# Batch 1's four-token sums by whole loads and GpSimd adds behind the first stage, 112-row value loads, and the last block's columns by segments

## The chip, the cores and the metric

The kernel runs on one core of a Trainium2 chip, in one launch. The metric is the device time of one execution in microseconds (us), lower is better. Engines are named as in the profile: PE (TensorE matmuls), PEld (its weight loads), DVE (VectorE), ACT (ScalarE), POOL (GpSimd) and SP, which here only issues DMAs.

## The reference, cut to what matters

Attention over 4 batches, 8 heads, 576 tokens, 64 dimensions, followed by two gated feed-forward networks over the 2304 tokens.

```python
q_d = q.reshape(B, H, Sd, 4, D).mean(axis=3)        # sums of 4 tokens: Sd = 144
k_d = k.reshape(B, H, Sd, 4, D).mean(axis=3)
v_d = v.reshape(B, H, Sd, 4, D).mean(axis=3)
out_up = np.repeat(sm_attn(q_d, k_d, v_d), 4, axis=2)
mask = np.abs(pos[:, None] - pos[None, :]) < 4      # and attention over 7 neighbours
out_local = softmax(where(mask, scale * q @ k.T, -1e9)) @ v
x = (out_up + out_local).transpose(0, 2, 1, 3).reshape(2304, 512)
x = (silu(x @ w_gate) * (x @ w_val)) @ w_out         # 512 -> 1536 -> 512
h = x @ w_in; return (h * clip(h + 3, 0, 6) / 6) @ w_out2   # 512 -> 2048 -> 512
```

The weights arrive as 64-bit floats; q, k and v are 32-bit.

## The kernel before

**Blocks and units.** The 2304 tokens are cut into five blocks of 512, 384, 512, 512 and 384 columns (`BLOCKS = [8, 6, 8, 8, 6]` units of 64). In each block PE runs 68 units of 12 matmuls (P: 9 where the block has 384 columns): G (gate), V (value), O (output of the first network), H and P (the second), in pairs of neighbours, G0 G1 V0 V1, then G2 G3 V2 V3 O0 O1 and so on. Each fp32 factor is split into a high and a low part, and a product is three matmuls. In block 0 the weights are also loaded as 64-bit words (512 KB per unit), their upper halves are gathered by ACT (`decode_a`, line 237, tile `top`), completed by DVE (`decode_b`, line 246, tile `w`), split into high (ACT, line 264) and low (DVE, line 269, tile `wr`, once for a pair of units), and the decoded copy is stored to DRAM (`kept`) for the later blocks. `prefetch(i)` runs these steps 8, 5, 4 and 3 units ahead of the unit that PE runs. Every engine works through its own instructions in the order in which they were issued.

**The first stage (`first_batch`).** Batch 0's attention is computed before block 0 starts, in the order that the string `FRONT` writes out by hand: two letters and numbers name a step, `T`, `E`, `R` for transposes, their evacuations and sums of 4, `SC`, `M`, `W`, `N`, `PT`, `Pa`, `Pd`, `V`, `Xh`, `Xl` for the windows of 96 tokens, `d.` for the attention over the sums, `to`, `de`, `hi`, `lo` for the first weights. `fill` inserts dummy matmuls. `load_vw(i)` loads the values of a window of 102 tokens with one DMA on SP's queue (window 0 and 5 with two), and step `V` reads them. The weights `pw` of a window stand in the tile `held` (tag `x2`, one buffer) until step `PT` has transposed them.

**Sums of 4 tokens of the later batches.** Batch b's sums (`dn["q"]`, `dn["k"]`, `dn["v"]`, 72 rows for each half) are needed while block b-1 runs. For batches 2 and 3 `down_sums` loads one token of the four with a DMA on POOL's queue and adds the other three with accumulating DMAs. For batch 1 two steps of `FRONT` do it in another way for q and k: `two` loads tokens 0 and 1 (512-byte pieces of two tokens, four DMAs of 288 KB into tiles that take over the tag `fnat`), `sums` adds tokens 2 and 3 with four accumulating DMAs and then folds each pair with one GpSimd addition (line 723); v's sums are eight DMAs behind unit 25 of block 0 (`SUMV`). PE transposes q's and k's sums behind units 9, 11, 13 and 15 of block 0 (`sums_T`, line 337, tiles `pqT`, `pkT`).

**Later attention.** From batch 1 on, scores and values of the 7 neighbours are computed on DVE between the units, chunk by chunk (`chunk_scores`, lines 852 and 855; `unit_values`, from line 889), from chunk loads on SP's queue (`load_chunk`, pool `ap`, which takes over the memory of the first stage's pool `fp`). `evac` and `put_cols` write a unit's 64 columns of x into `xr`.

**Output.** `put_out` evacuates 128 tokens of a block at a time from PSUM into `os` and stores them with one DMA on SP's queue; in the last block there are three, e = 0 and 2 evacuated by ACT (line 1075) and e = 1 by DVE (line 1073). The columns of a unit are ordered by token and then by the 16 segments of 36 tokens, so the store's destination has 8 tokens outermost.

Of the kernel before, what the change touches and what calls it, by code (L numbers as in the profile page):

```python
# [43 lines left out]
SUMV = 25  # L44
# [11 lines left out]
PT0 M2 to0 N1 M3 two dP2 to1 de0 Pd0 W3 dO0 dO3 dN0 dN3 dO2 N3 dO1 Pa0 W2 dN2 dN1 sums to2 PT1  # L56
# [6 lines left out]
def tile_kernel(  # L63
# [299 lines left out]
    def first_batch():  # L363
# [6 lines left out]
        with tc.tile_pool(name="fp", bufs=1) as fp:  # L370
# [82 lines left out]
            def load_vw(i):  # L453
# [243 lines left out]

            twos = {}

            def pairs(t):  # L700
                for w, src in (("q", q), ("k", k)):
                    for half in range(2):
                        if not t:
                            st = fp.tile([TT, GT, H // 2, D], F32, tag="fnat", name=f"two{w}{half}", bufs=4)
                            st = st.rearrange("p a h d -> p (a h d)")[:NJH, :2 * H * D]
                            twos[w, half] = st.rearrange("p (h t d) -> p h t d", h=H, t=2)
                        tok = src[1, :, half * NJH * 4:(half + 1) * NJH * 4, :]
                        tok = tok.rearrange("h (j t) d -> j h t d", t=4)[:, :, t:t + 2]
                        how = {"accum_op": ALU.add} if t else {}
                        tc.keep_in_program_order(nc.gpsimd.dma_start(twos[w, half], tok, **how))  # L710

            def two():
                tc.keep_in_program_order(nc.gpsimd.tensor_copy(consts[:QT, 60:61], nm[3][:QT, 0, :1]))
                pairs(0)

            def sums():
                pairs(2)
                for w in "qk":
                    dn[w] = sp.tile([NJH, 2, H, D], F32, tag="dn" + w, name=f"dn{w}1", bufs=1)
                    for half in range(2):  # L720
                        st = twos[w, half]
                        tc.keep_in_program_order(
                            nc.gpsimd.tensor_tensor(dn[w][:, half], st[:, :, 0], st[:, :, 1], op=ALU.add)
                        )
# [11 lines left out]
            def lo(i):  # L736
# [5 lines left out]
                "Pa": Pa, "Pd": Pd, "V": V, "Xh": Xh, "Xl": Xl, "sums": sums, "two": two,  # L742
# [44 lines left out]
    first_batch()  # L787
    front[0] = False
# [111 lines left out]
    def step_x(limit):  # L900
# [12 lines left out]
        def evac():  # L913
            xf = ap.tile([P, NC, 2, 2, NSEG], F32, tag="xf", name=f"xf{gu}")
            for tp in range(2):
                for par in range(2):
                    rows = slice(par * D, par * D + D)
                    nc.vector.tensor_tensor(  # L918
                        xf[rows, :, :, tp, :].rearrange("p c j s -> p j c s"),
# [4 lines left out]
            bi = max(m for m in range(NB) if starts[m] <= gu)  # L924
            put_cols(bi, (gu - starts[bi]) * UT, xf.rearrange("p c j t s -> p c (j t s)"))
# [140 lines left out]
    def put_out(bi, e, ps):  # L1066
# [5 lines left out]
        if e % 2 and bi == NB - 1:  # L1072
# [32 lines left out]
    for bi in range(NB):  # L1105
# [34 lines left out]
        for i in range(bi * NU, (bi + 1) * NU):  # L1140
# [74 lines left out]
```

## Time and profile before

| what | value |
|---|---|
| median of 3 runs | 947.93 us (946.87 to 948.83) |
| the profiled execution's own time | 947.45 us |
| its span | 945.7 us |
| PE busy | 932.0 us (99%) |
| DVE busy | 731.7 us (77%) |
| ACT busy | 505.3 us (53%) |
| POOL busy | 105.8 us (11%) |

The span is what the profile covers; the execution's own time is 1.75 us longer. A busy share is a mean over stages: the first stage ends at about 53 us, block 0 at about 254 us, blocks 1 to 4 follow. Times in the rows are from the span's start.

### The profile page before, as it was taken

The numbers are of one execution on the slowest core, as the hardware profiler recorded it, in microseconds if no ns is written. First come the engines' busy times: TensorE is split into PE (matmuls) and PEld (weight loads), VectorE is DVE, ScalarE is ACT, GpSimd is POOL, SyncE is SP. The second block draws the span as 40 slices with busy tenths as digits, with TensorE's granted clock in tenths as the row PEclk, the third lists the DMA queues.
The fourth block names the chain that finished last, engine by engine and source line by source line (L and its number), as shares of the span: only waits on it lengthen the run. The fifth ranks groups of instructions, "written<-read, shape, count | busy, mean of one in ns | idle before, by whom it ended". The sixth has DMA issues, their size and how long they took to land.

```text
span 945.7 us, 13226 instructions
## 1 busy us (share of the span) xinstructions
PE 932.0 (99%) x4945; PEld 793.7 (84%) x4945; DVE 731.7 (77%) x1067; ACT 505.3 (53%) x945; POOL 105.8 (11%) x117
## 2 busy tenths in 40 slices
PE   8999999999999999999999999999999999999997
PEld 6887887788899988978888778888888888999996
DVE  6969989798889979998835899995447994545652
ACT  5964677877534586453335764533335445434542
POOL 6420022000153100027300000000000000000000
PEclk9999999999999999999999999999999999999999
DMA  9898899678899732579932223542232224434331
GB/s 223 174 305 314 301 347 308 192 267 295 290 239 215 163 108 69 191 219 181 200 112 89 68 90 130 196 141 91 92 109 89 89 90 131 143 128 134 131 114 34
DMA packets 100048, 160.80 MB, mean 170 GB/s; under 512 B 53368, under 2 KB 57080, under 8 KB 99984
## 3 DMA queue, kind: packets, MB, share of 16 engines
q1 hardware_dynamic: 57680, 131.43, 43.6%
q0 software_dynamic: 37408, 10.71, 10.6%
q10 hardware_dynamic: 4896, 17.83, 4.7%
q8 instruction: 39, 0.64, 0.3%
q14 instruction: 25, 0.20, 0.1%
HBM read 137.31 MB, written 22.54 MB: 169 GB/s over the span
## 4 chain that ended last, share of the span: by engine, by line
PE 72%; DVE 11%; DMA 8%; ACT 4%; issue 3%; POOL 1%; SPq 1%; ACTq 0%; POOLq 0%; DVEq 0%
PE aO L1050 15%; PE pV L358 15%; PE aP L1050 14%; PE pG L358 14%; PE pH L358 12%; DMA twok<-in_k_dram 3%; DVE wr L269 2%; DMA k<-in_k_dram 2%; DMA w<-in_moe_w_out_dram 1%; DVE pv L889 1%; DVE xf L918 1%; DVE h L1024 1%; DVE gH L1026 1%; SPq L147 1%; DVE pv L893 1%
## 5 line engine op out<-in xcount | busy, mean ns | idle before, releaser
L269 DVE TENSOR_TENSOR wr<-w,wr 128x1024 fp32r<-128x1024 f32 x170 | 207.6, 1221 | 118.0 <-ACT wr L264 117.6
L264 ACT ACTIVATE wr<-w 128x1024 fp32r<-128x1024 f32 x170 | 179.4, 1056 | 117.7 <-issue 54.1
L1050 PE MATMUL aP<-wr,gH 128*128 128x512 f32 x864 | 211.4, 395 | 1.4 <-ACT gH L1025 0.8
L358 PE MATMUL pH<-x,wr 128*128 128x512 f32 (+1 forms) x960 | 211.3, 371 | 0.7 <-DVE wr L269 0.4
L358 PEld LDWEIGHTS pH<-x,wr 128*128 128x128 f32 x960 | 173.3, 188 | 26.0 <-issue 2.1
L1050 PEld LDWEIGHTS aP<-wr,gH 128*128 128x128 f32 x864 | 159.6, 188 | 36.2 <-ACT gH L1025 1.6
L358 PE MATMUL pG<-xr,wr 128*128 128x512 f32 (+1 forms) x720 | 153.6, 368 | 0.8 <-ACT xr L309 0.8
L358 PE MATMUL pV<-xr,wr 128*128 128x512 f32 (+1 forms) x720 | 153.4, 368 | 0.9 <-ACT sl L1014 0.9
L1050 PE MATMUL aO<-gV,wr 128*128 128x512 f32 (+1 forms) x720 | 152.7, 368 | 0.0
L358 PEld LDWEIGHTS pV<-xr,wr 128*128 128x128 f32 x720 | 130.9, 188 | 18.2 <-ACT sl L1014 1.4
L358 PEld LDWEIGHTS pG<-xr,wr 128*128 128x128 f32 x720 | 130.8, 188 | 18.3 <-ACT xr L309 1.2
L1050 PEld LDWEIGHTS aO<-gV,wr 128*128 128x128 f32 x720 | 130.8, 188 | 16.7
L1023 ACT ACTIVATE h<-pH,consts 128x512 f32<-128x512 f32 (+1 forms) x80 | 51.3, 642 | 52.7 <-PE pH L358 52.5
L1025 ACT ACTIVATE gV<-sl 128x512 fp32r<-128x512 f32 (+1 forms) x60 | 35.0, 584 | 67.5 <-DVE sl L1020 67.4
L1014 ACT ACTIVATE sl<-pG 128x512 f32<-128x512 f32 (+1 forms) x60 | 33.2, 554 | 70.5 <-PE pG L358 70.4
L1025 ACT ACTIVATE gH<-h 128x512 fp32r<-128x512 f32 (+1 forms) x80 | 46.8, 586 | 44.6 <-DVE h L1024 44.4
L237 ACT ACTIVATE top<-w 128x512 f16<-128x512 bf16 x68 | 53.3, 794 | 16.6 <-DVE w L246 4.7
L852 DVE TENSOR_TENSOR pr<-q,k 128x1792 f32<-128x1792 f32 x27 | 54.5, 2019 | 9.8 <-DMA k<-in_k_dram 9.7
L1024 DVE SCALAR_TENSOR_TENSOR h<-h,pH 128x512 f32<-128x512 f32 (+1 forms) x80 | 50.5, 631 | 13.3 <-ACT h L1023 12.6
L1026 DVE TENSOR_TENSOR gH<-h,gH 128x512 fp32r<-128x512 f32 (+1 forms) x80 | 50.5, 632 | 11.6 <-ACT gH L1025 11.5
L889 DVE TENSOR_TENSOR pv<-sc,v 128x1792 f32<-128x1792 f32 x27 | 54.6, 2021 | 0.5
L855 DVE TENSOR_REDUCE sc<-pr 128x28 f32<-128x1792 f32 x27 | 54.4, 2013 | 0.2
(137 smaller groups left out, 754.1 us busy)
## 6 DMA issues: line engine op xcount, KB each, us to landing
w<-kept SPq DMA_DIRECT2D x136, 512.0 KB
kept<-w ACTq DMA_DIRECT2D x34, 512.0 KB
w<-in_moe_w_out_dram SPq DMA_DIRECT2D x28, 512.0 KB
w<-in_moe_w_in_dram SPq DMA_DIRECT2D x16, 512.0 KB
w<-in_moe_w_gate_dram SPq DMA_DIRECT2D x12, 512.0 KB
w<-in_moe_w_val_dram SPq DMA_DIRECT2D x12, 512.0 KB
out_dram<-os SPq DMA_DIRECT2D x16, 256.0 KB
dnv<-in_v_dram POOLq DMA_DIRECT2D x24, 144.0 KB, 7.1
```

The lines of the kernel that those rows point to most:

```text
L237: behind(nc.scalar.activation(halves(top[i % 2], 2, F16)[:, :, 1], h3.bitcast(BF16), AF.Copy))
L264: behind(nc.scalar.activation(parts[i][:, 0], w32[i // 2].rearrange("p u e -> p (u e)"), AF.Copy))
L269: behind(nc.vector.tensor_tensor(r[:, 1], s, r[:, 0].bitcast(F32), op=ALU.subtract))
L358: nc.tensor.matmul(ps, r[:, a, c], x[:, c, b_, :ps.shape[1]], start=part is HIGH and a == c == 0, stop=part is LOW and c == NC - 1,)
L852: nc.vector.tensor_tensor(pr, qt[:, a:a + SUB, None, :].to_broadcast([P, SUB, W, D]), win(kt, a, SUB), op=ALU.mult)
L855: nc.vector.tensor_reduce(sc[:, a:a + SUB], pr, axis=AX.X, op=ALU.add)
L889: nc.vector.tensor_tensor(pr, pe[:, a:a + SUB, :, None].to_broadcast([P, SUB, W, D]), win(vt, a, SUB), op=ALU.mult)
L1023: nc.scalar.activation(h, ps, AF.Relu, scale=1 / 6, bias=half1[:, 0:1])
L1024: nc.vector.scalar_tensor_tensor(h, h, 1.0, ps, op0=ALU.min, op1=ALU.mult)
L1025: nc.scalar.activation(g[:, 0, :nt], h, AF.Copy)
L1026: nc.vector.tensor_tensor(g[:, 1, :nt], h, g[:, 0, :nt].bitcast(F32), op=ALU.subtract)
L1050: nc.tensor.matmul(ps, **one, start=f_ == 0 and a == b_ == 0, stop=f_ == nf - 1 and b_ == 1,)
```

## The change

Batch 1's sums of 4 tokens leave `FRONT` (steps `two`, `sums`) and unit 25. A new function `whole_sums`, called right behind the first stage, loads all four tokens of a half of q, k or v with one DMA on POOL's queue (1 KB pieces, 576 KB), six in all, two of them ahead, into two halves of one tile with the tag `x2`; GpSimd then folds the four tokens with two additions per piece. The values of batch 0's windows are loaded with 112 rows where 112 fit (96 and then 3 in the last window), and rows outside the sequence are zeroed by DVE and not loaded. In the last block the columns of two neighbouring units are ordered by segment first, so that `put_out` stores with 16 segments outermost; the last 128 tokens are evacuated half by DVE, half by ACT.

```diff
-SUMV = 25
 FRONT: ... -PT0 M2 to0 N1 M3 two dP2 to1 de0 Pd0 W3 ... dO1 Pa0 W2 dN2 dN1 sums to2 PT1
            +PT0 M2 to0 N1 M3 dP2 to1 de0 Pd0 W3 ... dO1 Pa0 W2 dN2 dN1 to2 PT1
     def put_cols(bi, col, xv):
-        dst = columns(bi, col, xv)
+        dst = columns(bi, col, UT)
+        if bi == NB - 1:
+            e, r = divmod(col // UT, 2)
+            dst = columns(bi, e * P, P).rearrange("p c a (s u t) -> p c a s u t", s=NSEG, u=2)[:, :, :, :, r]
+    def whole_sums(b):
+        st = sp.tile([P, NC, 2, UMAX * UT], F32R, tag="x2", name=f"st{b}", bufs=1).bitcast(F32)
+        st = st.rearrange("p c a t -> p (c a t)")[:NJH].rearrange("p (g h t d) -> p g h t d", g=2, h=H, t=4)
+        gp = Ordered(nc.gpsimd)
+        pieces = [(w, half) for w in "qkv" for half in range(2)]
+        def load(n):
+            w, half = pieces[n]
+            src = {"q": q, "k": k, "v": v}[w][b, :, half * NJH * 4:(half + 1) * NJH * 4, :]
+            gp.dma_start(st[:, half], src.rearrange("h (j t) d -> j h t d", t=4))
+        def add(n):
+            w, half = pieces[n]
+            if half == 0:
+                dn[w] = sp.tile([NJH, 2, H, D], F32, tag="dn" + w, name=f"dn{w}{b}", bufs=1)
+            t = st[:, half]
+            gp.tensor_tensor(t[:, :, 0:2], t[:, :, 0:2], t[:, :, 2:4], op=ALU.add)
+            gp.tensor_tensor(dn[w][:, half], t[:, :, 0], t[:, :, 1], op=ALU.add)
+        load(0)
+        load(1)
+        for n in range(len(pieces)):
+            add(n)
+            if n + 2 < len(pieces):
+                load(n + 2)
             def load_vw(i):
                 if lo < 0:
-                    late(nc.sync, t[:-lo], v[0, :, :-lo, :].rearrange("h s d -> s h d"))
+                    nc.vector.memset(t[:-lo], 0.0)
                 if hi > S:
-                    late(nc.sync, t[S - lo:hi - lo], v[0, :, S - (hi - S):, :].rearrange("h s d -> s h d"))
+                    nc.vector.memset(t[QT:], 0.0)
                 a, e = max(lo, 0), min(hi, S)
-                late(nc.sync, t[a - lo:e - lo], v[0, :, a:e, :].rearrange("h s d -> s h d"))
+                m = QT if hi > S else min(QT + 16, P, S - a)
+                late(nc.sync, t[a - lo:a - lo + m], v[0, :, a:a + m, :].rearrange("h s d -> s h d"))
+                if a + m < e:
+                    late(nc.sync, t[a - lo + m:e - lo], v[0, :, a + m:e, :].rearrange("h s d -> s h d"))
...
-            def pairs(t): ...   def two(): ...   def sums(): ...
     first_batch()
+    whole_sums(1)
     def evac():
+            by = "p c (s j t) -> p c j t s" if bi == NB - 1 else "p c (j t s) -> p c j t s"
+            xs = xf.rearrange(by, j=2, t=2, s=NSEG)
...
     def put_out(bi, e, ps):
-        if e % 2 and bi == NB - 1:
+        if bi == NB - 1 and e == BLOCKS[bi] * UT // P - 1:
+            h = DM // 2
+            nc.vector.tensor_copy(os[:, :h], ps[:, :h])
+            nc.scalar.activation(os[:, h:], ps[:, h:], AF.Copy)
+        elif e % 2 and bi == NB - 1:
...
+            elif bi == NB - 1:
+                dst = flat(out, (b * S + u * 4) * DM, [[SL * DM, NSEG], [DM, 4 * m], [1, DM]])
             else:
                 dst = flat(out, (b * S + u * 4) * DM, [[DM, 4 * m], [SL * DM, NSEG], [1, DM]])
...
-            if i == SUMV:
-                last = [t for key, t in state.items() if key[0] == "g"][-1]
-                for _ in down_sums(1, ["v"], last[:, 0, :1].bitcast(F32)):
-                    pass
```

## Rows read from the trace of the kernel before

**Rows 1.** Timeline, PE: start, length, tiles, [idle before <-releaser], first stage and block 0.

```profile
48.82 0.88 PE L159 MATMUL fO<-turned,vw 102*64 102x96 f32 x16 [0.38 <-DMA vw<-in_v_dram]
...
80.59 0.41 PE L337 MATMUL pqT<-ident,dnq 72*128 72x72 f32 x4
80.81 5.71 PE L358 MATMUL pG<-xr,wr 128*128 128x512 f32 x24
...
87.66 6.07 PE L358 MATMUL pV<-xr,wr 128*128 128x512 f32 x24 [0.88 <-ACT sl L1014]
93.56 0.42 PE L337 MATMUL pkT<-ident,dnk 72*128 72x72 f32 x4
```

**Rows 2.** Busy time by stretch, block 0: length, each engine's busy us, clock, DMA share, GB/s.

```profile
54.00:90.00 36.00, 35.12 (x160) 28.90 (x159) 28.87 (x31) 20.96 (x30) 3.05 (x2) 1.00 0.93 306
90.00:122.00 32.00, 32.00 (x146) 26.06 (x146) 31.03 (x38) 20.39 (x31) 0.00 (x0) 1.00 0.88 310
```

**Rows 3.** Timeline, DVE: low halves of the weights and the first scores.

```profile
70.75 2.02 DVE L852 TENSOR_TENSOR pr<-q,k 128x1792 f32<-128x1792 f32 x1 [2.46 <-DMA k<-in_k_dram]
...
78.78 1.23 DVE L269 TENSOR_TENSOR wr<-w,wr 128x1024 fp32r<-128x1024 f32 x1
...
86.20 1.22 DVE L269 TENSOR_TENSOR wr<-w,wr 128x1024 fp32r<-128x1024 f32 x1
```

**Rows 4.** Timeline, POOL: additions of the first stage, sums of batch 1.

```profile
16.07 1.26 POOL L446 TENSOR_TENSOR spread<-spread 72x512 f32<-72x512 f32 x1 [5.95 <-DMA spread<-in_v_dram]
17.42 0.72 POOL L447 TENSOR_TENSOR fvd<-spread 72x256 f32<-72x256 f32 x1
...
29.61 1.86 POOL L710 DMA_DIRECT2D twoq<-in_q_dram  x2 [0.40 <-PE fPT L159]
...
36.41 1.41 POOL L710 DMA_DIRECT2D twoq<-in_q_dram  x1 [3.33 <-DMA twoq<-in_q_dram]
...
46.06 1.27 POOL L723 TENSOR_TENSOR dnq<-twoq 72x512 f32<-72x512 f32 x1 [1.20 <-DMA twoq<-in_q_dram]
...
61.85 1.75 POOL L723 TENSOR_TENSOR dnk<-twok 72x512 f32<-72x512 f32 x1 [1.09 <-DMA twok<-in_k_dram]
```

**Rows 5.** Timeline, DVE: instructions beside POOL's additions, and one without.

```profile
46.45 1.42 DVE L246 SCALAR_TENSOR_TENSOR w<-w,top 128x512 int32<-128x512 int32 x1
...
60.34 0.97 DVE L246 SCALAR_TENSOR_TENSOR w<-w,top 128x512 int32<-128x512 int32 x1 [2.03 <-ACT top L237]
...
62.98 1.18 DVE L246 SCALAR_TENSOR_TENSOR w<-w,top 128x512 int32<-128x512 int32 x1
...
64.69 0.68 DVE L246 SCALAR_TENSOR_TENSOR w<-w,top 128x512 int32<-128x512 int32 x1
```

**Rows 6.** Groups of DVE's instructions by line, 54 to 90 us: busy us, mean ns.

```profile
L855 DVE TENSOR_REDUCE sc<-pr 128x28 f32<-128x1792 f32 x2 | 4.0, 2010 | 0.0
...
L1020 DVE TENSOR_TENSOR sl<-sl,pV 128x512 f32<-128x512 f32 x4 | 2.7, 677 | 0.0
```

**Rows 7.** Timeline, SP: DMA issues of the values and of the first chunk.

```profile
16.02 22.06 SPq L147 DMA_DIRECT2D vw<-in_v_dram  x8
...
63.64 0.33 SPq L147 DMA_DIRECT2D q<-in_q_dram  x1
```

**Rows 8.** Timeline, ACT and SP at the end, and a 128x256 evacuation of the first stage.

```profile
53.86 0.37 ACT L159 ACTIVATE xr<-fO 128x256 fp32r<-128x256 f32 x1
...
937.20 3.32 SPq L1084 DMA_DIRECT2D out_dram<-os  x3
...
939.29 0.60 ACT L1075 ACTIVATE os<-aP 128x512 f32<-128x512 f32 x1 [2.12 <-PE aP L1050]
```

**Rows 9.** Busy time by stretch at the end, columns as in rows 2.

```profile
936.00:940.00 4.00, 3.25 (x15) 2.36 (x13) 0.69 (x1) 1.20 (x2) 0.00 (x0) 1.00 0.18 31
940.00:944.00 4.00, 0.00 (x0) 0.00 (x0) 0.00 (x0) 0.00 (x0) 0.00 (x0) 0.89 0.50 159
944.00:946.00 2.00, 0.00 (x0) 0.00 (x0) 0.00 (x0) 0.00 (x0) 0.00 (x0) 0.50 0.03 12
```

More of the change, by code (lines that the diff above doesn't have):

```diff
@@ L55 @@
 SC0 dM1 M0 Rk3 dE1 Rk2 dT0 dP0 W0 SC1 dS3 dM3 dT1 dP1 SC2 M1 dE3 W1 dS2 dT3 N0 dM2 dP3 SC3 dE2 dT2
-PT0 M2 to0 N1 M3 two dP2 to1 de0 Pd0 W3 dO0 dO3 dN0 dN3 dO2 N3 dO1 Pa0 W2 dN2 dN1 sums to2 PT1
+PT0 M2 to0 N1 M3 dP2 to1 de0 Pd0 W3 dO0 dO3 dN0 dN3 dO2 N3 dO1 Pa0 W2 dN2 dN1 to2 PT1
 Pa1 Pd1 SC5 SC4 M5 W5 PT3 V1 M4 N2 Pa3 de1 Xh1 W4 V0 Xh0 Pd3 Xl1 N5 de2 PT2 V3 Pd2 Pa2 Xl0 to3 PT5 Xh3
@@ L298, in tile_kernel, with columns @@
     x_done = [0]
-    def columns(bi, col, xv):
+    def columns(bi, col, n):
         if bi not in xr:
             xr[bi] = sp.tile([P, NC, 2, UMAX * UT], F32R, tag="xr", name=f"xr{bi}")
-        return xr[bi][:, :, :, col:col + xv.shape[2]]
+        return xr[bi][:, :, :, col:col + n]
     def put_cols(bi, col, xv):
-        dst = columns(bi, col, xv)
+        dst = columns(bi, col, UT)
+        if bi == NB - 1:
+            e, r = divmod(col // UT, 2)
+            dst = columns(bi, e * P, P).rearrange("p c a (s u t) -> p c a s u t", s=NSEG, u=2)[:, :, :, :, r]
         nc.scalar.activation(dst[:, :, 0], xv, AF.Copy)
@@ L684, in X @@
                         e = min(QT, starts[bi + 1] * UT - t0)
-                        yield bi, cs, columns(bi, t0 + a - starts[bi] * UT, ps[:, :, a:e]), ps[:, :, a:e]
+                        yield bi, cs, columns(bi, t0 + a - starts[bi] * UT, e - a), ps[:, :, a:e]
                         a = e
@@ L696, in Xl @@
                         vec.tensor_tensor(to[:, cs, 1], xv, to[:, cs, 0].bitcast(F32), op=ALU.subtract)
[L698 to L724, printed above, removed]
             def to(i):
@@ L741, in first_batch @@
                 "dN": dN, "SC": SC, "M": M, "W": W, "N": N, "PT": PT,
-                "Pa": Pa, "Pd": Pd, "V": V, "Xh": Xh, "Xl": Xl, "sums": sums, "two": two,
+                "Pa": Pa, "Pd": Pd, "V": V, "Xh": Xh, "Xl": Xl,
                 "Yh": lambda i: Xh(i, False), "Yl": lambda i: Xl(i, False), "to": to, "de": de, "hi": hi, "lo": lo,
@@ L913, in evac @@
         def evac():
-            xf = ap.tile([P, NC, 2, 2, NSEG], F32, tag="xf", name=f"xf{gu}")
+            bi = max(m for m in range(NB) if starts[m] <= gu)
+            xf = ap.tile([P, NC, UT], F32, tag="xf", name=f"xf{gu}")
+            by = "p c (s j t) -> p c j t s" if bi == NB - 1 else "p c (j t s) -> p c j t s"
+            xs = xf.rearrange(by, j=2, t=2, s=NSEG)
             for tp in range(2):
@@ L918, in evac @@
                     nc.vector.tensor_tensor(
-                        xf[rows, :, :, tp, :].rearrange("p c j s -> p j c s"),
+                        xs[rows, :, :, tp, :].rearrange("p c j s -> p j c s"),
                         px[tp * D:tp * D + D, :, :, par, :],
@@ L923, in evac @@
                     )
-            bi = max(m for m in range(NB) if starts[m] <= gu)
-            put_cols(bi, (gu - starts[bi]) * UT, xf.rearrange("p c j t s -> p c (j t s)"))
+            put_cols(bi, (gu - starts[bi]) * UT, xf.rearrange("p c (s t) -> p c s t", t=4) if bi == NB - 1 else xf)
             x_done[0] += 1
```

## The prediction

> **What bounds the kernel now.** I read the page's busy times first, then PE's timeline for its idle places, then DVE and POOL around them, then the end. PE is busy for 932.0 of 945.7 us, so a change gains or loses only at the few places where PE waits or has ended. The first is window 5's value step, 0.38 us late for its DMA [rows 1]. In block 0 there is one stall, 0.88 us before V4 at 87.66 [rows 1]. The reader should see how thin block 0's lead is: DVE is busy for 28.87 of 36 us from 54 to 90 us and for 31.03 of 32 from 90 to 122 [rows 2], and it finishes the low half of a pair of weights just before PE wants it. For the pair G4 G5 it is done at 78.78 + 1.23 = 80.01 and PE starts at 80.81; for V4 V5 it is done at 87.42 and PE starts at 87.66 [rows 1, 3]. So DVE sets PE's pace here, with a lead of 0.8 and 0.2 us. The last place is the end: PE has ended at 939.3, and the last store moves data until 944 [rows 8, 9].
>
> **The first stage.** The steps `two` and `sums` issue eight DMAs and four additions on POOL; all of it leaves. PE waits for none of these there. What PE waits for is the value load. SP needs 22.06 us to issue eight value loads [rows 7], and the last one makes PE wait 0.38 us [rows 1]. Seven loads stand there now; if they are spread better over the engines, this wait goes: -0.4. Bounds: 0 if the wait stays, -1.1 if the 0.74 us that an addition of `sums` holds DVE there (below) also counts; PE's row after row up to 48.44 shows no other wait, so I take -0.4. The two zeroings on DVE have no input and run before the first transposes have landed, and the rows beyond 102 are read by nobody: nothing.
>
> **What GpSimd's additions cost.** An addition of 512 elements takes 1.26 us, one of 256 takes 0.72 [rows 4], so 256 elements more cost 0.54, and one of 1024 is estimated at 1.26 + 2 x 0.54 = 2.34. A piece is one of 1024 and one of 512: 3.6 us, six pieces 21.6 us, in place of four additions of 1.27 (5.1 us).
>
> When: the tile has the tag of `held`, which PE reads until 48.4, so the first load is issued there. The first 288 KB load of `two` was issued at 29.61 and had landed when POOL went on at 36.41 [rows 4], 6.8 us; so the first addition begins at about 55. A piece can't follow faster than its additions and one issue (0.93, half of 1.86 in rows 4), 4.5 us, so six pieces fill 55 to 82 at best and about 55 to 90 if POOL is held up too. That is the stretch in which DVE sets the pace.
>
> How the two engines meet is shown by three instructions of line 246, both of whose inputs are in SBUF: 0.68 us alone, but 1.42 at 46.45, 0.97 at 60.34 and 1.18 at 62.98, each while an addition runs [rows 5]. The addition of 46.06 ends at 47.33, and the instruction ends 0.54 later: DVE had waited for the addition to end. It is so in the other direction too: the addition of 61.85 takes 1.75, since it waits for the line-269 instruction before it [rows 4]. The three lose 0.74 + 0.29 + 0.50 = 1.53 us to 5.1 us of additions: 30%.
>
> Bounds for 21.6 us. From below: 30% of it is 6.5; before already pays 0.8 of it behind 54 us, and DVE's wait of 2.46 us for the first chunk [rows 3] is swallowed by a late DVE (its load stood behind `sums` on SP at 63.64 [rows 7], which goes too); 3.2 stay. From above: of the 36 us from 54 to 90, DVE is idle for 7.1 and for 4.0 + 2.7 [rows 6] runs instructions that read one tile of SBUF or PSUM; the rest, 22.2 less the 0.8 of holding, is 21.4 us that exclude an addition. 21.4 + 21.6 = 43.0 us can't run side by side; with the free 13.8 us all used by additions DVE is 43.0 - 36 = 7.0 us late, with half of them used 13.9. I take 7.0: the 30% come from stretches where DVE had pauses, and against the 13.9 speaks that a held-up POOL drifts into whatever DVE leaves free. Less the lead of 0.3 (between 0.2 and 0.8, nearer the smaller, since DVE gets no pause until 122) PE is 6.7 us late; bounds 2.9 and 13.6. It isn't made up: PE's work behind it is fixed, and the stalls of before that it could swallow are 0.9 at 87.66.
>
> The Trainium skill (SBUF — State Buffer, "SBUF: two separate sides") says that DVE and GpSimd share one pair of ports under an exclusive lock, held for the whole instruction, and that a DVE instruction with two SBUF inputs needs it. The three rows agree. By that rule taken alone the lower bound would be the 7.0 of full exclusion and not 3.2; the sum above stands without it.
>
> **What else moves in block 0.** POOL's queue holds only these loads and additions; nothing else waits behind them until block 1's sums at 254. PE transposes q's sums at 80.59 and k's at 93.56 in order [rows 1]; with q done at about 65 and k at about 75 neither waits. The `x2` tile is wanted again at the end of O, over 60 us later. The same bytes of q, k and v are loaded either way, now closer together in a stretch where the DMA engines are at a share of 0.93 [rows 2]; a late DVE also asks for weights later, so I add nothing, and count it in the range. v's eight DMAs at 130 to 165 go: PE waits for none of them.
>
> **The end.** The last evacuation takes 0.60 for 512 columns [rows 8]; a 256-column one 0.37, its DVE counterpart about the same: -0.2. Then the stores: 4 us x 31 + 4 x 159 + 2 x 12 GB/s = 784 KB, the three of 256 KiB, at a share of 0.50, so with half of the 16 DMA engines [rows 9]. At that share the first 4 us hold 1.44 us of transfer, so data flow from 938.56, 1.36 behind the first issue at 937.20. If 16 segments outermost use all engines, the last store, issued at 939.7, flows from 941.06 at 318 GB/s and is through in 0.82, at 941.9 and not 944.1: -2.2 with the evacuation's 0.2. I take -2.0; bounds -0.2 (rate unchanged) and -2.4. The reordered columns cost DVE and ACT only other strides in blocks 3 and 4, where PE shows no wait: nothing.
>
> The Trainium skill (DMA: Bandwidth & Descriptors, "Why a DMA increments its semaphore by 16 and not by 1") says that a hardware-queue DMA runs on the largest number of engines up to 16 that divides the outermost size on both sides. For 8 and 128 that is 8, which the share of 0.50 agrees with; it would be 16 now, and 6 and 16 for 102 and 112 rows, which no row here shows.
>
> **Sum.** 947.45 + 6.7 - 0.4 - 2.0 = 951.75 against the profiled execution; the median of the runs is 0.48 above it: 952.2 us, 0.45% slower.
>
> **The rivals.**
> - The other side: POOL's additions fit into what DVE leaves free, and DVE is less than 0.3 us late. For it: DVE's pauses between 54 and 61, the vanished wait of 2.46, and a lock that DVE might win each time. Against it: 21.6 us don't fit into 13.8. It would give 947.9 - 2.4 = 945.5. It decides from a lateness below 2.7 (0.3 + 0.4 + 2.0): then the change is a gain. Chance of over 0.2% faster: 0.21.
> - The lateness is near its lower bound of 3.2 (1 to 4.5), and both ends cancel: 2.9 - 2.4 gives 948.4. Chance 0.18.
> - Loads or additions are so late that PE waits for k's sums at 93.56: with DMAs twice as large at the pace of rows 4 (13.6 us each, two in flight) k is done at about 84, and only a starved POOL adds more. Some 5 us on top of the forecast: 957. Chance 0.06.
> - That the stores or value loads don't spread better takes away 1.8 and 0.4 of the gain; it moves the forecast to 954.4 and lies within its range.
>
> **How the numbers follow.** The forecast, lateness from 4.5 to 13, has 0.55; its own range is 949.9 to 957. About 0.2%, 1.9 us, is what a measurement of this kernel can tell from no change. Slower is 0.55 + 0.06 = 0.61, same 0.18, faster 0.21. To leave out 2 in 10 the range goes from the other side's 945.3 to 957.
>
> **What the profile will show.** Right: additions of about 2.3 and 1.3 us on POOL from 55 to 90; instructions of lines 246, 269, 852 and 1026 lengthened beside them; PE waits before G4, V4 or O0 that sum to some 7 us; no wait at window 5; a DMA share near 1 at the end, which comes 2 us sooner behind PE. Wrong, if DVE's lengthened instructions sum to under 3 us, or if PE runs through 60 to 110 without waits.

## The result, and the profile after

The changed kernel takes 957.37 us (956.13 to 961.82 over six runs) against 948.38 of the kernel before on the same chip: a ratio of 1.0098, with an interval of 1.0073 to 1.0122. That is slower, as forecast, but by 9.0 us and not by 4.3, and 0.4 us beyond the end of the range. Ratios and their intervals are formed from undisturbed executions alone, medians from all. The profiled execution has a span of 956.8 us, 11.1 more than before: the two profiled executions (958.47 and 947.45 us) lie 2 us farther apart than the medians, and the terms below are read from these two.

PE's timeline of the changed kernel, rows with a wait and those that answer to [rows 1]; its L386 and L1056 are L358 and L1050 of before:

```profile
53.14 5.72 PE L386 MATMUL pG<-xr,wr 128*128 128x512 f32 x24
...
66.47 5.80 PE L386 MATMUL pG<-xr,wr 128*128 128x512 f32 x24 [2.18 <-DVE sl L1026]
...
79.07 5.53 PE L1056 MATMUL aO<-gV,wr 128*128 128x512 f32 x23 [1.14 <-DVE wr L268]
84.44 0.41 PE L365 MATMUL pqT<-ident,dnq 72*128 72x72 f32 x4
...
85.95 5.51 PE L386 MATMUL pG<-xr,wr 128*128 128x512 f32 x23 [0.77 <-DVE wr L268]
...
95.17 0.50 PE L386 MATMUL pV<-xr,wr 128*128 128x512 f32 x1 [3.14 <-ACT sl L1020]
98.06 7.93 PE L386 MATMUL pV<-xr,wr 128*128 128x512 f32 x23 [2.39 <-DVE wr L268]
105.83 0.41 PE L365 MATMUL pkT<-ident,dnk 72*128 72x72 f32 x4
```

Block 0 begins 0.12 us earlier than before (53.14 for 53.26), and k's first transposes, a fixed place in PE's order, come 12.27 us later (105.83 for 93.56). So block 0 has lost 12.4 us, and the whole loss is there: PE ends 12.7 us later than before, and the end behind PE, 6.45 us before, is 4.87. The five waits sum to 9.62 us, in place of the 0.88 at 87.66: 8.7 more. A further 2.4 us is in the row of 98.06: its 23 matmuls take 7.93 us, while the 23 of 85.95 take 5.51. The remaining 1.2 us are spread over PE's restarts behind the waits.

Windows of the changed kernel, columns as in [rows 2], at PE's last wait and at the end:

```profile
60.00:90.00 30.00, 25.92 (x114) 20.42 (x114) 26.25 (x21) 12.36 (x18) 20.82 (x13) 1.00 0.99 307
...
96.00:98.00 2.00, 0.00 (x0) 0.00 (x0) 2.00 (x2) 0.39 (x1) 1.92 (x2) 0.61 0.98 382
98.00:100.00 2.00, 1.94 (x5) 1.55 (x6) 2.00 (x3) 0.27 (x1) 1.15 (x1) 0.50 0.49 191
100.00:102.00 2.00, 2.00 (x6) 1.59 (x5) 2.00 (x2) 2.00 (x4) 0.00 (x0) 0.50 0.58 101
102.00:104.00 2.00, 2.00 (x7) 1.55 (x6) 2.00 (x3) 0.80 (x2) 0.00 (x0) 0.68 1.00 400
...
951.00:955.00 4.00, 0.93 (x5) 0.43 (x3) 0.72 (x2) 0.38 (x1) 0.00 (x0) 1.00 0.69 190
955.00:957.00 2.00, 0.00 (x0) 0.00 (x0) 0.00 (x0) 0.00 (x0) 0.00 (x0) 0.90 0.04 13
```

The clock column explains the slow row of 98.06. PE ran one matmul between 92.03 and 98.06, and the granted clock fell to 0.50, which is 1.2 GHz, and was back at 1.00 (2.4 GHz) from 104. The first line says that the DMA engines were full in block 0 too, at a share of 0.99 from 60 to 90 us (before, 0.93 from 54 to 90 [rows 2]). The two last lines answer to [rows 9]: a DMA share of 0.69 in the last 4 us of transfer where it was 0.50.

DVE's timeline, instructions of block 0 beside the additions (L245, L268, L856 and L1032 are L246, L269, L852 and L1026 of before), and those of 67.33 and 84.67, which ran beside none or between two:

```profile
57.49 2.43 DVE L245 SCALAR_TENSOR_TENSOR w<-w,top 128x512 int32<-128x512 int32 x1 [2.32 <-ACT top L236]
60.22 1.42 DVE L245 SCALAR_TENSOR_TENSOR w<-w,top 128x512 int32<-128x512 int32 x1 [0.29 <-ACT top L236]
61.55 4.17 DVE L268 TENSOR_TENSOR wr<-w,wr 128x1024 fp32r<-128x1024 f32 x1
...
67.33 0.68 DVE L1032 TENSOR_TENSOR gV<-sl,gV 128x512 fp32r<-128x512 f32 x1
...
75.08 2.80 DVE L856 TENSOR_TENSOR pr<-q,k 128x1792 f32<-128x1792 f32 x1 [3.53 <-DMA k<-in_k_dram]
...
84.67 1.23 DVE L268 TENSOR_TENSOR wr<-w,wr 128x1024 fp32r<-128x1024 f32 x1
85.81 2.88 DVE L1032 TENSOR_TENSOR gV<-sl,gV 128x512 fp32r<-128x512 f32 x1
...
95.38 2.63 DVE L268 TENSOR_TENSOR wr<-w,wr 128x1024 fp32r<-128x1024 f32 x1
```

POOL's timeline beside it, from five of the six pieces:

```profile
56.98 2.39 POOL L158 TENSOR_TENSOR st<-st 72x1024 f32<-72x1024 f32 x1 [5.62 <-DMA st<-in_q_dram]
59.45 1.63 POOL L158 TENSOR_TENSOR dnq<-st 72x512 f32<-72x512 f32 x1
61.38 0.83 POOL L158 DMA_DIRECT2D st<-in_k_dram  x1 [0.30 <-POOL dnq L158]
62.23 2.41 POOL L158 TENSOR_TENSOR st<-st 72x1024 f32<-72x1024 f32 x1
...
67.16 0.83 POOL L158 DMA_DIRECT2D st<-in_k_dram  x1 [0.30 <-POOL dnq L158]
72.26 2.38 POOL L158 TENSOR_TENSOR st<-st 72x1024 f32<-72x1024 f32 x1 [4.27 <-DMA st<-in_k_dram]
74.72 1.28 POOL L158 TENSOR_TENSOR dnk<-st 72x512 f32<-72x512 f32 x1
...
85.69 2.46 POOL L158 TENSOR_TENSOR st<-st 72x1024 f32<-72x1024 f32 x1 [1.57 <-DMA st<-in_v_dram]
...
97.00 2.15 POOL L158 TENSOR_TENSOR dnv<-st 72x512 f32<-72x512 f32 x1
```

Read the two together. The L1032 instruction starts at 85.81, 0.12 us behind POOL's addition of 85.69, and ends at 88.69, 0.54 us behind that addition's end (88.15), as the one at 46.45 did in [rows 5]. It took 2.88 us instead of 0.68. The Trainium skill (SBUF — State Buffer, "SBUF: two separate sides") says that whichever of the two engines starts first has the shared ports for its whole instruction. These rows agree, in both directions: a 512-element addition that finds DVE at work takes 1.63 or 2.15 us, for 1.28 at 74.72. DVE's instructions with one input from SBUF at most are not lengthened: in the stretch of the groups below L859 (one SBUF input) has a mean of 2006 ns and L1026 (one SBUF and one PSUM input) of 675, and before they had 2009 and 677.

DVE's groups of the same four lines from 53 us to the same place in PE's order (pV at 133.69, and at 121.47 before):

```profile
L245 DVE SCALAR_TENSOR_TENSOR w<-w,top 128x512 int32<-128x512 int32 x25 | 22.6, 918 | 3.9 <-ACT top L236 3.9
L268 DVE TENSOR_TENSOR wr<-w,wr 128x1024 fp32r<-128x1024 f32 x12 | 19.0, 1581 | 0.4 <-ACT wr L263 0.4
L856 DVE TENSOR_TENSOR pr<-q,k 128x1792 f32<-128x1792 f32 x5 | 10.8, 2169 | 3.5 <-DMA k<-in_k_dram 3.5
...
L1032 DVE TENSOR_TENSOR gV<-sl,gV 128x512 fp32r<-128x512 f32 x8 | 7.6, 954 | 0.0
```

They sum to 60.0 us; the same 25, 12, 5 and 8 instructions took 17.5 + 14.6 + 10.1 + 5.5 = 47.7 before. DVE is held for 12.3 us, and PE loses 12.4. That the two agree so closely is in part chance, since 2.4 of PE's 12.4 are the clock. DVE's idle time before these lines hardly changed: 3.9 + 0.4 + 3.5 = 7.8 us, and 4.6 + 0.8 + 2.5 = 7.9 before. From this profile alone one would say that the additions are the whole cause and the loads cost nothing. The experiments say otherwise.

The end, SP's issues, DVE and ACT (answers to [rows 8]):

```profile
949.87 3.50 SPq L1096 DMA_DIRECT2D out_dram<-os  x3
...
951.97 0.42 DVE L1080 COPY os<-aP 128x256 f32<-128x256 f32 x1 [0.67 <-PE aP L1056]
952.42 0.38 ACT L1081 ACTIVATE os<-aP 128x256 f32<-128x256 f32 x1 [2.58 <-DVE os L1080]
```

The two halves of the last evacuation follow each other. The last data is in SBUF 0.87 us behind PE's end, where one ACT instruction had needed 0.64.

### The profile page after: what moved, and what is told of

The parts are those of the page before. It is cut to its first block, busy times and chain, and to the rows that moved or that the text cites. A ratio compares the mean times of both kernels' runs of the same rounds, so it can differ in the third digit from the quotient of the medians.

```text
span 956.8 us, 13203 instructions
## 1 busy us (share of the span) xinstructions
PE 936.0 (98%) x4945; PEld 795.3 (83%) x4945; DVE 746.6 (78%) x1070; ACT 505.2 (53%) x945; POOL 110.0 (12%) x113
## 4 chain that ended last, share of the span: by engine, by line
PE 78%; DVE 11%; ACT 4%; issue 3%; DMA 3%; SPq 1%; ACTq 0%; DVEq 0%
PE aP L1056 16%; PE pH L386 14%; PE pV L386 14%; PE aO L1056 14%; PE pG L386 14%; DVE wr L268 3%; DMA w<-in_moe_w_val_dram 1%; DVE pv L893 1%; PE fO L158 1%; DVE xf L925 1%; DVE pv L897 1%; DVE gH L1032 1%; DVE h L1030 1%; DMA w<-kept 1%; ACT pd L764 1%
## 5 line engine op out<-in xcount | busy, mean ns | idle before, releaser
L268 DVE TENSOR_TENSOR wr<-w,wr 128x1024 fp32r<-128x1024 f32 x170 | 212.0, 1247 | 117.5 <-ACT wr L263 117.1
L386 PE MATMUL pH<-x,wr 128*128 128x512 f32 (+1 forms) x960 | 211.5, 372 | 0.8 <-DVE wr L268 0.4
L1056 PE MATMUL aP<-wr,gH 128*128 128x512 f32 x864 | 211.2, 395 | 0.8 <-DVE wr L268 0.5
L386 PEld LDWEIGHTS pH<-x,wr 128*128 128x128 f32 x960 | 173.3, 188 | 26.2 <-issue 2.1
L1056 PEld LDWEIGHTS aP<-wr,gH 128*128 128x128 f32 x864 | 159.7, 188 | 35.4 <-issue 1.6
L386 PE MATMUL pV<-xr,wr 128*128 128x512 f32 (+1 forms) x720 | 155.7, 372 | 5.5 <-ACT sl L1020 3.1
L386 PE MATMUL pG<-xr,wr 128*128 128x512 f32 (+1 forms) x720 | 154.3, 369 | 3.7 <-DVE sl L1026 2.2
L1056 PE MATMUL aO<-gV,wr 128*128 128x512 f32 (+1 forms) x720 | 153.0, 368 | 1.1 <-DVE wr L268 1.1
L386 PEld LDWEIGHTS pV<-xr,wr 128*128 128x128 f32 x720 | 132.7, 190 | 23.3 <-ACT sl L1020 3.3
L386 PEld LDWEIGHTS pG<-xr,wr 128*128 128x128 f32 x720 | 130.6, 188 | 22.2 <-issue 2.6
L1056 PEld LDWEIGHTS aO<-gV,wr 128*128 128x128 f32 x720 | 130.7, 188 | 18.2 <-DVE wr L268 1.6
L856 DVE TENSOR_TENSOR pr<-q,k 128x1792 f32<-128x1792 f32 x27 | 55.3, 2048 | 8.7 <-DMA k<-in_k_dram 8.5
L1032 DVE TENSOR_TENSOR gH<-h,gH 128x512 fp32r<-128x512 f32 (+1 forms) x80 | 50.5, 632 | 11.6 <-ACT gH L1031 11.5
L245 DVE SCALAR_TENSOR_TENSOR w<-w,top 128x512 int32<-128x512 int32 x68 | 51.6, 771 | 9.5 <-ACT top L236 6.4
```

What stands on the lines that cost most here:

```text
L245: behind(nc.vector.scalar_tensor_tensor(w32[i // 2][:, i % 2].bitcast(I32), h12, 13, top[i % 2], op0=ALU.logical_shift_right, op1=ALU.bitw ...
L268: behind(nc.vector.tensor_tensor(r[:, 1], s, r[:, 0].bitcast(F32), op=ALU.subtract))
L386: nc.tensor.matmul(ps, r[:, a, c], x[:, c, b_, :ps.shape[1]], start=part is HIGH and a == c == 0, stop=part is LOW and c == NC - 1,)
L856: nc.vector.tensor_tensor(pr, qt[:, a:a + SUB, None, :].to_broadcast([P, SUB, W, D]), win(kt, a, SUB), op=ALU.mult)
L1032: nc.vector.tensor_tensor(g[:, 1, :nt], h, g[:, 0, :nt].bitcast(F32), op=ALU.subtract)
L1056: nc.tensor.matmul(ps, **one, start=f_ == 0 and a == b_ == 0, stop=f_ == nf - 1 and b_ == 1,)
```

## The experiments

The table lists every run, with the kernel before's median on the same chip. "k at" is when PE starts k's first transposes in the profile (93.56 before, 105.83 after), and "end" the span behind PE's last matmul.

| kernel | us | before | ratio (interval) | k at | end |
|---|---|---|---|---|---|
| e1 ends only | 945.65 | 948.06 | 0.9966 (0.9947-0.9985) | 92.68 | 4.79 |
| e2 few additions | 954.60 | 948.06 | 1.0063 (1.0042-1.0085) | 101.72 | 4.79 |
| e3 additions, no loads | 958.79 | 948.06 | 1.0097 (1.0068-1.0126) | 107.06 | 4.83 |
| e4 v as before | 952.95 | 948.06 | 1.0051 (1.0032-1.0070) | 98.59 | |
| e5 early, few additions | 949.28 | 948.02 | 1.0011 (0.9992-1.0031) | 97.17 | |
| e6 early, all additions | 956.88 | 948.02 | 1.0084 (1.0062-1.0106) | 104.28 | |
| e7 a third of the additions | 949.04 | 948.02 | 1.0004 (0.9983-1.0024) | 98.24 | |
| e8 ends, ACT last | 944.14 | 948.02 | 0.9948 (0.9931-0.9965) | 92.27 | 4.64 |
| e9 early q and k, few additions | 944.28 | 946.69 | 0.9974 (0.9964-0.9984) | 92.43 | |
| e10 values only | 946.11 | 946.69 | 0.9996 (0.9987-1.0005) | 91.77 | 6.57 |
| e11 last block only | 945.98 | 946.69 | 0.9996 (0.9979-1.0013) | 93.00 | 4.55 |
| e12 two half stores | 944.47 | 946.69 | 0.9977 (0.9963-0.9992) | | 4.36 |

**e1, the change without the new sums.** The rest of the change stays; `two`, `sums` and the v step of before return.

```diff
-    whole_sums(1)
+    # FRONT has "two" and "sums" again, the loop its SUMV step
```

> The changed kernel with batch 1's sums put back as before (steps two and sums in the first stage, v's accumulating DMAs behind unit 25); the 112-row value loads, the last block's columns and the split last evacuation stay. Theory L (GpSimd's additions hold DVE up while they run) and theory D (the six whole loads crowd the DMA engines, so weights and the first chunk come late) both put the whole loss in the sums: 946.3 to 947.2, 1.2 to 2.1 us below before, of which 1.6 at the end (from 6.45 us to 4.87 between PE's end and the span's end) and 0.1 in the first stage. Theory E (the reordered columns or the value loads cost something in blocks 3 and 4 or in the first stage): 950 or more.

It gains: 2.4 us by the medians. PE has no wait in block 0. So the new sums cost 957.37 - 945.65 = 11.7 us by the medians (12.5 by the two ratios), and not the 6.7 of the forecast.

**e2, the loads without the additions.** The additions run on one of 64 elements of each head; the rest of the sums is a constant, so the kernel leaves most of the sums out.

```diff
-gp.tensor_tensor(t[:, :, 0:2], t[:, :, 0:2], t[:, :, 2:4], op=ALU.add)
-gp.tensor_tensor(dn[w][:, half], t[:, :, 0], t[:, :, 1], op=ALU.add)
+gp.tensor_tensor(t[:, :, 0:2, :1], t[:, :, 0:2, :1], t[:, :, 2:4, :1], op=ALU.add)
+gp.tensor_tensor(dn[w][:, half, :, :1], t[:, :, 0, :1], t[:, :, 1, :1], op=ALU.add)
...
+    gp.memset(dn[w], 0.01)
```

> The changed kernel, but GpSimd adds only one of the 64 dimensions of each piece (16 and 8 elements per row and not 1024 and 512); the sums are otherwise a constant that GpSimd writes before the first load, so most of the sums is left out. All six whole loads stay, with their waits. L: DVE is no longer held, PE's waits between 60 and 100 us go to under 2 us and the clock stays at 2.4 GHz: 946.3 to 948.5. D: the loads are as before, so weights and the first chunk are still late: 953 or more.

That additions are the whole cause fell here: the loads alone cost 9.0 us over e1. DVE is no longer held (a mean of 687 ns for L245, where the changed kernel has 918), but waits. DVE's timeline of e2 has the first chunk of k:

```profile
76.23 2.03 DVE L857 TENSOR_TENSOR pr<-q,k 128x1792 f32<-128x1792 f32 x1 [6.28 <-DMA k<-in_k_dram]
```

DVE's timeline of e1, the same instruction:

```profile
69.90 2.03 DVE L884 TENSOR_TENSOR pr<-q,k 128x1792 f32<-128x1792 f32 x1 [1.80 <-DMA k<-in_k_dram]
```

SP's timelines, the issue of that load, in e2:

```profile
61.69 0.44 SPq L146 DMA_DIRECT2D k<-in_k_dram  x1
```

and in e1:

```profile
62.19 0.42 SPq L147 DMA_DIRECT2D k<-in_k_dram  x1
```

So from the issue to the use of k it is 14.5 us in e2 and 7.7 in e1.

ACT's timeline of e2, the longest wait for weights:

```profile
81.66 0.79 ACT L236 ACTIVATE top<-w 128x512 f16<-128x512 bf16 x1 [7.66 <-DMA w<-in_moe_w_gate_dram]
```

Windows of e2, before the loads and in them:

```profile
30.00:50.00 20.00, 20.00 (x268) 18.21 (x267) 17.88 (x43) 17.60 (x77) 0.69 (x1) 1.00 0.52 157
...
60.00:90.00 30.00, 24.75 (x100) 19.06 (x99) 18.09 (x21) 12.08 (x17) 5.01 (x13) 0.94 1.04 322
```

The DMA engines are half idle from 30 to 50 us and full from 60 to 90 (the share is a mean that can come out above 1). The rate, 322 GB/s, is that of e1 in the same stretch (317), so nothing is slower; other bytes move. The DMA queues from 60 to 90 us (packets, MB, share), SP's in e1:

```profile
q1 hardware_dynamic: 2901, 6.87, 69.6%
```

SP's and POOL's in e2:

```profile
q1 hardware_dynamic: 2103, 5.40, 58.9%
q0 software_dynamic: 818, 2.30, 27.7%
```

SP's queue brings block 0's own k chunk and weights, and 1.5 MB less of them gets through beside the 2.3 MB of POOL's loads; in e1 POOL's queue moves nothing there. One thing is not as in the changed kernel: without additions POOL issues its last load at 75.16 and not at 83.29, so the loads stand closer together, and 9.0 us is their price at that pace. The clock adds to it: after a wait of 2.14 us, 23 matmuls at 79.44 take 7.14 us.

**e3, the additions without the loads.** e1, with twelve additions of the same sizes on a tile of zeros, back to back from 63.72 us (in the changed kernel they are spread from 57 to 99); their result is read by nobody.

```diff
...
+gp.memset(st[:, 0], 0.0)
+for n in range(6):
+    t = st[:, 0]
+    gp.tensor_tensor(t[:, :, 0:2], t[:, :, 0:2], t[:, :, 2:4], op=ALU.add)
+    gp.tensor_tensor(st[:, 1, :, 0], t[:, :, 0], t[:, :, 1], op=ALU.add)
```

> e1_ends_only with twelve GpSimd additions of the sizes of the change (six of 1024, six of 512 elements per row) on a scratch tile of zeros behind the first stage, with no load: extra work that nothing reads, about 22 us on GpSimd from 64 us on. L: DVE's two-input instructions beside them are held for 8 to 12 us, PE waits as much less its lead: 953 to 957. D: nothing waits for these additions and no byte more is moved: within 0.7 us of e1_ends_only.

The additions alone cost 13.1 us over e1 (958.79, above the 953 to 957 expected), with a DMA share of only 0.42 and 0.29 from 70 to 90 us. DVE has no idle time from 70 to 100. DVE's timeline of e3, one of L269's:

```profile
79.40 3.38 DVE L269 TENSOR_TENSOR wr<-w,wr 128x1024 fp32r<-128x1024 f32 x1
```

POOL's timeline of e3, all twelve:

```profile
63.72 28.84 POOL L159 TENSOR_TENSOR sti<-sti 72x1024 f32<-72x1024 f32 x12
```

Unhindered they would take 6 x (2.38 + 1.28) = 22.0 us by the rows above, so POOL is held for 6.8 us as well.

9.0 and 13.1 sum to 22.1, and the two together cost 11.7 to 12.5. They overlap: while DVE is held it would have waited for its data anyway, and its wait for k is 3.53 us in the changed kernel where e2 has 6.28. By these runs the pair costs no more than the additions alone.

**e4, v as before.** Only q and k are loaded whole and added.

```diff
-pieces = [(w, half) for w in "qkv" for half in range(2)]
+pieces = [(w, half) for w in "qk" for half in range(2)]
+# and the SUMV step of before for v
```

> The changed kernel with v's sums as before (accumulating DMAs behind unit 25), so four pieces and not six: 14.6 us of additions, which end at about 83 us. L: in the changed kernel DVE's holding before 83 us made PE some 5 us late (PE waits 2.2, 1.1 and 0.8 up to 86, the larger ones behind it), and the clock doesn't fall: 950.5 to 953. D: four of six loads, which stand just as close together: 953 to 955.

Two thirds of the pieces cost 1.0051 - 0.9966 = 0.85% of 948 us, 8.1 us, and the last third 4.4. Within the intervals the cost follows the number of pieces, so it isn't the one late piece that the third rival spoke of.

**e5, e2's loads in the first stage.** Quarters of 4 heads go through the tiles of before's `two`, four loads ahead, from 32 us on; the additions are cut, and most of the sums left out, as in e2.

```diff
+quarters = [(w, half, hh) for w in "qkv" for half in range(2) for hh in range(2)]
 ...
 def two():
+    ...
+    for n in range(4):
+        load_q(n)
 def sums():
+    for n in range(12):
+        add_q(n)
+        if n + 4 < 12:
+            load_q(n + 4)
```

> e2_few_adds with the same bytes in the same 1 KB pieces loaded earlier: twelve loads of half the size on POOL's queue, in the first stage from 29 us on, four ahead, into the tiles that two used; GpSimd adds only one of 64 dimensions and the rest of the sums is a constant, so most of the sums is left out. Theory D1 (e2's loss of about 9 us against e1_ends_only comes from where the loads stand: from 49 to 85 us the DMA share is full and the first chunk and the weights queue beside them, while from 30 to 50 us the share is 0.4 to 0.6): 945.5 to 949. Theory D2 (loads of this kind on POOL's queue cost that much wherever they stand): 952 or more.

Of the 9.0 us, 4.3 stay (1.0011 - 0.9966), and DVE still waits 4.3 us for k. This time it is not the transfer of k. The quarters stand in memory of the first stage's pool, which the chunk's tiles take over, so SP waits 6.3 us for v's last quarter to land, at 67.7 us, and 0.9 us for POOL to read it, before it can issue the chunk. SP's timeline of e5:

```profile
69.28 0.42 SPq L147 DMA_DIRECT2D k<-in_k_dram  x1
```

That is 7.1 us later than in e1, and the weights behind it in SP's queue are late with it; from issue to use k takes 5.2 us here, less than e1's 7.7.

**e6, e5 with all additions.**

```diff
-t = whole.pop(n)[:, :, :, :1]
+t = whole.pop(n)[:, :, :, :64]
...
```

> e5_early_few_adds with all additions (24 on GpSimd of 512 and 256 elements per row, about 24 us, from 36 us on), so the complete sums. If only the place of the loads mattered: within 1 us of e5_early_few_adds. L: the additions hold DVE in the first stage, where it is busy for 9 of 10 us, and behind it, and the first chunk's load waits for the last addition: 951 to 958.

The additions cost 6.9 us on top of e5 (1.0084 - 1.0011). On 12 x (1.27 + 0.72) = 23.9 us of additions that is 29%, in a kernel that already waits. Moving them does not hide them, since DVE's work is on PE's path in the first stage too. PE's timeline of e6:

```profile
47.54 0.54 PE L159 MATMUL fPT<-ident,held 96*102 96x96 f32 x4 [1.88 <-DVE turned L159]
```

The first stage ends 5.3 us later than in e1 (its last transposes begin at 58.16, not 52.83), and of the 11.6 us by which k's transposes are late only 6.3 arise in block 0, where SP can issue the chunk of k only at 76.35, behind the last addition.

**e7, a third of e3's additions.** The 1024-element ones are left out, six of 512 stay.

```diff
-gp.tensor_tensor(t[:, :, 0:2], t[:, :, 0:2], t[:, :, 2:4], op=ALU.add)
```

> e3_adds_no_loads with only the six smaller of the twelve additions that nothing reads (512 elements per row): about 8 us on GpSimd from 64 us on and not 21.6. L, with DVE's lateness in proportion to the additions (e3_adds_no_loads was 13 us over e1_ends_only for 28.8 us on POOL): 949 to 951. If DVE's lead and its pauses swallow this much: within 1 us of e1_ends_only.

6 x 1.28 = 7.7 us of additions cost 1.0004 - 0.9966 = 0.38%, 3.6 us, that is 47%; e3's 22.0 us cost 12.4 by the ratios, 56%. The 3.6 us are uncertain by some 2.7, so a free third is excluded, and a smaller free amount is not.

**e9, e5 for q and k alone**, v as before, which tells apart what is left in e5.

```diff
-quarters = [(w, half, hh) for w in "qkv" for half in range(2) for hh in range(2)]
+quarters = [(w, half, hh) for w in "qk" for half in range(2) for hh in range(2)]
```

> e5_early_few_adds for q and k alone (eight loads and not twelve, the last landed at about 58 us), v's sums as before by accumulating DMAs; GpSimd adds one of 64 dimensions of q and k, the rest of these sums is a constant, so most of them is left out. D1: e5_early_few_adds was still 3.6 us over e1_ends_only because its v loads stood from 50 to 68 us, where the DMA share was 1.0; without them 945.5 to 946.5, as e1_ends_only. If the remaining 3.6 us come from the loads of q and k: 948.5 or more.

The remainder is gone: k's transposes stand at 92.43, as in e1, and SP issues the chunk of k at 61.90. Windows of e9 in the same two stretches as e2's:

```profile
30.00:50.00 20.00, 20.00 (x269) 18.21 (x268) 18.21 (x43) 17.70 (x78) 11.05 (x22) 1.00 0.98 224
...
60.00:90.00 30.00, 29.76 (x137) 24.30 (x136) 27.56 (x29) 18.08 (x28) 0.00 (x0) 1.00 0.93 317
```

q's and k's whole loads cost nothing from 31 to 53 us, where the DMA engines have room without them (e2's first line). Behind the first stage the six loads cost 9.0 us (e2). v's whole loads at a place where nothing waits for them or for their memory were not run.

**e10 and e11, the two other parts alone.** e10 is the kernel before with the 112-row value loads; e11 the kernel before with the last block's columns, its last tile evacuated by ACT alone.

```diff
 # e10, on before (cut)
-late(nc.sync, t[a - lo:e - lo], v[0, :, a:e, :].rearrange("h s d -> s h d"))
+m = QT if hi > S else min(QT + 16, P, S - a)
+late(nc.sync, t[a - lo:a - lo + m], v[0, :, a:a + m, :].rearrange("h s d -> s h d"))
...
 # e11, on before (cut)
+dst = flat(out, (b * S + u * 4) * DM, [[SL * DM, NSEG], [DM, 4 * m], [1, DM]])
```

> The kernel before with the 112-row value loads alone. If the gain of e1_ends_only over before (2.4 to 3.2 us) is 1.6 of the end and the rest of the value loads, which free SP's queue and the DMA engines in the first stage: 946.6 to 947.3, with no wait at window 5 and a smaller stall before V4 V5. If only the 0.38 us of the wait at window 5 count: 947.6, not to be told from before.

> The kernel before with the last block's column order alone, the last 128 tokens evacuated by ACT. The end behind PE shrinks from 6.45 to about 4.6 us: 946.0 to 946.5. Together with e10_values_only this should make up e8_ends_act_last.

By the times neither can be told from no change. By the profiles e10 has no wait at window 5 nor before V4, and the long end (6.57); e11 has the short end (4.55) and keeps a wait of 1.11 us in block 0. But e11, with the old loads, has no wait at window 5 either. The two ratios together make 0.9992, in agreement with e12's 0.9977 on the same chip, which has both parts, and not with e8's 0.9948 on another; that difference stays open.

**e8 and e12, the last evacuation.** e8 is e1 with ACT alone; e12 has an own tile and an own store for each half, ACT's first.

```diff
 # e8
-nc.vector.tensor_copy(os[:, :h], ps[:, :h])
-nc.scalar.activation(os[:, h:], ps[:, h:], AF.Copy)
+nc.scalar.activation(os, ps, AF.Copy)
 # e12
+nc.scalar.activation(right, ps[:, h:], AF.Copy)
+nc.vector.tensor_copy(os[:, :h], ps[:, :h])
+...
```

> e1_ends_only with the last 128 tokens evacuated by ACT alone, as before. In the changed kernel ACT's half begins only when DVE's half has ended (0.42 and 0.38 us one behind the other, where 0.60 stood). If they are one behind the other in every run, ACT alone ends 0.2 to 0.3 us sooner behind PE's end, and the time is that of e1_ends_only less 0.25, which the timing can't resolve and the profile's last rows can. If the halves did run side by side elsewhere: 0.2 later.

> e8_ends_act_last with the last 128 tokens evacuated in two halves into two tiles, ACT's first, each half stored by a DMA of its own (ACT's and SP's queue, 1 KB rows). If it was the common output tile that put the halves one behind the other in the changed kernel, they now run side by side and the end shrinks by 0.2 to 0.4 us. If it is the common PSUM tile that they read, DVE's half now waits for ACT's: within 0.3 us of e8_ends_act_last.

DVE's timeline of e12:

```profile
941.45 0.42 DVE L1110 COPY os<-aP 128x256 f32<-128x256 f32 x1 [1.14 <-ACT osr L1109]
```

Even with separate output tiles the second half waits for the first, now DVE for ACT. What the halves still share is the PSUM tile that both read. e8's end is 0.15 us shorter than e1's, and e8, at 0.9948, is the fastest by its ratio: faster than the kernel before by an interval that excludes 1. Between e1, e8 and e12 the intervals overlap.

## Why the prediction was right in direction and wrong in size

- **Additions on DVE: the term that made the time miss.** Right in kind and place: additions of 2.4 and 1.3 to 2.2 us on POOL, from 57 to 99 us, and the four lines lengthened beside them. The size was low. The step that I chose between the bounds, 7.0 us "with the free 13.8 us all used by additions", measured 12.3, near the 13.9 for half of that time used. Of the 6.7 us by which the profiled execution missed the forecast for it (958.47 for 951.75), 5.7 are in block 0 (12.4 for 6.7); the rest is the end (0.4), the first stage (0.3) and 0.4 of PE's later work. The argument against 13.9, that "a held-up POOL drifts into whatever DVE leaves free", failed: e3's POOL runs back to back and DVE has no idle time left from 70 to 100 us. Nor was DVE's wait of 2.46 us for the first chunk "swallowed by a late DVE": it became 3.53. The 30% from [rows 4, 5] became 56% (12.3 of 22.0 us); as a cost in time it is 47% in e7 and 56% in e3. They came from additions of 1.27 us with pauses of DVE around them; behind the new ones of 2.4 us a 0.68-us instruction loses up to 2.2 us (85.81), and an L268 of 1.23 us 2.9 (61.55). Which of the two differences, the pauses or the length of the additions, made the share grow was not isolated.
- **The loads.** "The same bytes of q, k and v are loaded either way, now closer together", "so I add nothing": this step was wrong as well, and that it hardly cost the forecast anything is luck. The bytes are the same, but before they moved in part from 30 to 50 us and from 130 on; now all move from 50 to 95, beside block 0's k chunk and weights. e2 prices that at 9.0 us, alone, and e9 shows for q and k that it is the place and not the loads. Beside the additions it is not seen, since DVE's idle time is 7.8 us for 7.9. But the loads paced the additions: POOL waited 1.6 to 4.7 us for each of the last four, so a piece came every 5 to 10 us and not every 4.5, and the additions ended at 99 us and not at 82 to 90.
- **How they add.** The changed kernel pays 11.7 to 12.5 us for both. A sum of the two right terms would have been too dear by 10 us. In its profile the loads' part is nearly invisible, because a late DVE finds its data there.
- **The clock.** Not foreseen. Of the 12.4 us, 2.4 are matmuls at a granted clock of 0.50 behind waits of 3.14 and 2.39 us. Here a long stall cost more than its length.
- **The first stage.** The wait at window 5 is gone, and SP issues the values in 14.06 us for 22.06. That it brings 0.4 us isn't shown: e11 has no such wait with the old loads either, and block 0 begins at 53.39 in e8 with the new loads and at 52.70 in e11 with the old ones. The wait of 0.88 us before V4, which I left as it is, goes with the new loads, by one profile of each run: e1, e8 and e10 don't have it, e11 does.
- **The end.** Forecast -2.0, measured 6.45 - 4.87 = 1.58 shorter. The store's part was right: without the split evacuation e8 and e11 have 4.64 and 4.55, 1.8 to 1.9 shorter for the -1.8 forecast. The evacuation's -0.2 was +0.2, since the halves run one behind the other. On the stores the Trainium skill (DMA: Bandwidth & Descriptors, "Why a DMA increments its semaphore by 16 and not by 1") gives 16 engines for 16 segments outermost and 8 before; the share of 0.69, in place of 0.50, agrees.
- **The rivals.** The other side fell: the additions didn't fit into DVE's pauses, nor did a third of them (e7). The second fell with it. The third had nearly the right time, 957, for a wrong reason: PE never waits for k's sums. k's last addition ends at 82.99, near the rival's own 84, and its transposes start at 105.83.

By its terms: 947.45 + 12.4 (block 0) - 0.1 (its earlier start) + 0.4 (the rest of PE's work) - 1.6 = 958.55, for the 958.47 of the profiled execution.

## What to carry to other kernels

An engine that shares ports with the engine that sets the pace is not free, however idle its row of the profile is: here its work cost about half of its own time where that engine had no slack (e3, e7), and it still cost 6.9 us when moved to an earlier stage (e6). Before moving loads, look at the DMA share of the place they go to and at who waits for data there; the share of the place they leave contains their own part (from 30 to 50 us it was 1.04 before and is 0.51 without them). And when two suspected costs delay the same engine, run each alone: the profile of both together shows only the one that ends last.

## What the runs showed that I had not expected

- One instruction was held before an addition ran. L268 at 61.55 took 4.17 us where it takes 1.23 alone. POOL's addition began only at 62.23; from 61.38 to 62.21 POOL was issuing a DMA. With the addition's end at 64.64 and its own 1.23 us behind that, the instruction would end about where it does, 65.72, so it seems held from its start. An issue alone does not hold DVE: L1032 at 67.33 ran within POOL's issue of 67.16 in its usual 0.68 us. So what held L268 before 62.23 is open.
- Two engines that evacuate halves of one PSUM tile work one behind the other in this program, 0.42 and then 0.38 us, whatever tile they write to (the changed kernel, e1 and e12). The profile names the other engine's copy as what each second half waited for, which it takes from the program's semaphores, so the program asked for this order. Whether the chip would need it no run shows.
- The granted clock of 0.50 outlasted the stall: it stood until 102 us, 4 us after PE had its work back.
